# Three edits in a one-core attention and two-MLP kernel: left tiles 32 bytes lower, score matmuls of two heads by turns, seven conversion slots dropped

## The chip, the cores and the metric

The kernel runs on one core of a Trainium2 chip. The metric is the time of one execution on the device in microseconds, as the median of several runs. A core has TensorE (PE in the profile; its weight loads are PEld), VectorE (DVE), ScalarE (ACT), GpSimd (POOL) and SyncE (SP, which here issues nearly all DMAs).

## The reference

Windowed attention (window 64, causal), then two MLPs, all in float32. It is cut here to what is computed:

```python
# q, k, v: (4, 8, 576, 64)
scores = np.matmul(q, k.transpose(0, 1, 3, 2)) / np.sqrt(64)
mask = (rel >= 0) & (rel < 64)          # rel = query position - key position
attn = softmax(np.where(mask, scores, -1e9))
x = matmul(attn, v)                      # -> (2304, 512)
x = np.maximum(x @ w_in, 0.0) ** 2 @ w_out          # (512, 2048), (2048, 512)
h = x @ w_in2
out = np.where(h > 0, h, np.exp(np.minimum(h, 0)) - 1) @ w_out2
```

## The kernel before

Work goes by five blocks of tokens (512, 256, 512, 512, 512). Every large product is made of three matmuls of `fp32r` halves (high by high, high by low, low by high), so operands are kept as a high and a low part, which ScalarE (`gs<-g`, `xo<-xq`, copy of the high part) and VectorE (the low part) make.

**First stage** (to about 307 us): attention of all blocks, and the first MLP of the first three blocks in the direct way: `h_chunk` (TensorE `ph<-xs,w`) and `o_chunk` (TensorE `o<-gs,w`). All of it follows `ORDER1`, an order written out by hand; while `pinned` is set, every instruction is queued on its engine behind the one before. Heads come in pairs, head 0 in partitions 0 to 63 and head 1 in 64 to 127. The action `S` (and from the second block on `G`) makes the scores: `s_half` (L551) has for each quarter `i` of 128 queries two matmuls of 64 rows by 64 columns, one for each half window, with 128 columns moving, in full fp32. In the trace these are `pa<-kr,qd`, two rows for each call. In the first block an `S` is for one head, with its own place in the order; elsewhere `act_S` (L1101) calls `s_half` for head 0 and then for head 1, into two PSUM banks. VectorE (`R`), ScalarE (`E`) and the rest of the softmax follow per quarter.

**Second stage** (307 to about 436 us): the first MLP of the last two blocks by a Strassen scheme. `stepw(p, i)` makes product `i` of step `p` (8 steps, products 1, 2, 6, 5, 7, 4, 3) from `xo` and weights that `w0_load` fetches; TensorE rows are `px<-xo,w` (products 1, 6, 7, 4) and `py<-xo,w` (2, 5, 3), 6 matmuls each. Products 5 and 3 of a step go into the same bank, y: after 5 and 7 are done, VectorE adds bank y and the kept `tl` into `gb`, and only then may product 3 write the bank. `outw` (rows `o<-gs,w`, 12 matmuls) comes between, and from 436 to 476 us 14 of them without a break. The products' order on TensorE is fixed by `in_turn`; the other engines' order is made by a planner, except where `tc.issue_after` sets it.

**Third stage** (from 476 us): the second MLP by the same scheme on 384 columns, with rows `px`, `py`, `po`.

**Portions.** Meanwhile the weights of the second MLP have to be decoded from 8-byte words, summed and split. That is the generator `portions()` (L437): a chain of small steps on ScalarE (`top<-tl`, `wo<-y`, `tl<-y`) and VectorE (`y<-tl,top`, `y<-y`, `wo<-y,wo`, `tl<-y,tl`) through one buffer `y`, with fetches (`tl<-in_moe`) and stores (`wd<-wo`, `wd<-tl`) on SP's queue. It has 433 steps: 73 in its first loop, then 19 for each of eight tasks of the first weight matrix and 26 for each of eight of the second. `ORDER1` takes 215 of them one by one (`P.0` to `P.214`; the last 19 stand at its end, behind all of its matmuls). The other 218 are taken by `slot()` (L516), which runs steps to the next place where the generator gives a non-zero value, and queues them behind the last VectorE and ScalarE instruction of the step before. 43 slots use them up; 66 slots are called.

**Places.** Pools are laid from both ends of SBUF. From the left: `cst` (with the pad `pad2`), `wts`, then `at` and later `lw` and `la`. From the right: `pad`, then `sc`, `xp` and later `gb`. In bytes of a partition, the first tile behind `cst` (`top`) begins at 2848. Every operand of a large product on the left (`w`, `wr`, `xo`, and `g` of the third stage) begins a whole multiple of 512 bytes above that; on the right `xs` begins at 179968 and `gs` at 212736, and all operands there lie multiples of 512 bytes apart. 179968 - 2848 is 345 x 512 + 480.

Of the kernel before, what the change touches and what calls it, by code (L numbers as in the profile page):

```python
# [10 lines left out]
F32 = mybir.dt.float32  # L11
# [8 lines left out]
P = 128  # L20
WIN = 64
# [114 lines left out]
def window_attention_then_two_mlps(  # L136
# [37 lines left out]
    vec, act, pe = Noted(nc.vector, "cd"), Noted(nc.scalar, "ca"), Noted(nc.tensor, "pe")  # L174
# [13 lines left out]
    D = P // 2  # L188
# [12 lines left out]
    cst = ctx.enter_context(tc.tile_pool(name="cst", bufs=1))  # L201
# [6 lines left out]

    pad = pool(ctx, "pad", 1, side="right")
    pad.tile([P, 56], F32, name="pad")  # L210
    cst.tile([P, 32], F32, name="pad2")

    wts = pool(ctx, "wts", 1)
    ps_o = pool(ctx, "ps_o", 1, space=PSUM)
# [286 lines left out]
    def slot(n=1):  # L501
        with tc.issue_after(last["cd"].ins), tc.issue_after(last["ca"].ins):
            quiet.append(1)
            while True:
                x = next(todo, None)
                if x is None:
                    count[0] += 1
                if x != 0:
                    break
            quiet.pop()  # L510
# [38 lines left out]

    st = {}  # L550

    def s_half(u, a, ps):
        t, p = u
        qr, kr = raw[u]["q"], raw[u]["k"]
        d = slice(a * D, (a + 1) * D)
        for i in range(BLOCKS[t] // P):
            for c in range(2):
                o = (2 * i + c) * WIN
                pe.matmul(
                    out=ps[c * WIN:(c + 1) * WIN, i * P:(i + 1) * P],  # L560
                    lhsT=qr[d, o:o + WIN], rhs=kr[d, o:o + P], start=True, stop=True,
                )
        st.setdefault(u, {})["s", a] = ps

    def s_max(u, a, g):
        t, p = u
# [140 lines left out]
    order = [(t, p) for t in range(NB) for p in range(HP)]  # L707
# [143 lines left out]
    def bank(k):  # L851
        if k == "x":
            return among((0, 1), "px")
        if k == "a":
            return among((2, 3), "py")
        return ps_o.tile([P, 512], F32, tag=f"o{k}", name="po")
# [4 lines left out]
    def in_turn(fn, *a):  # L861
        with ExitStack() as line:
            for ins in behind2:
                line.enter_context(tc.issue_after(ins.ins))
            fn(*a)
        behind2[:] = [last["pe"]]
# [22 lines left out]
    def w0_load(m=1):  # L889
        for p, n in SEQW[wl0[0]:wl0[0] + m]:  # L890
            k = PROD[n][0]
            w = W[-1, p, k] = lw[0].tile([P, 2, HW], F32R, tag="ring", name="w0", bufs=10)
            sp.dma_start(out=w.bitcast(F32), in_=wd0[p][:, ORD1.index(k)])
        wl0[0] += m

    def square(g):
        act.activation(out=g, in_=g, func=AF.Relu)
        act.activation(out=g, in_=g, func=AF.Square)

    def ready(j, f):  # L900
        s = gw[j] = sc.tile([P, 2, NMAX], F32R, tag="gs", name="gs", bufs=GB)
        split(s[:, 0], s[:, 1], f, vec)

    def stepw(p, i):

        if i == 1:
            QW[p] = {"x": bank("x"), "done": set()}
        q = QW[p]
        k = "x" if i in (1, 6, 7, 4) else "z" if i == 2 else "y"
        if i in (2, 5):  # L910
            q[k] = bank("a")
        in_turn(prod, -1, p, i, q[k], i in (1, 2, 5), i in (4, 2, 3), NMAX)
        w0_load()
        q["done"].add(i)
        if i in (1, 6, 7):
            act.activation(out=tl[i], in_=q["x"], func=AF.Copy)
        if i == 2:
            f = sc.tile([P, NMAX], F32, tag="g", name="g")
            add(f, tl[1], q["z"])
            square(f)  # L920
            ready(p, f)
        if i == 4:
            f = sc.tile([P, NMAX], F32, tag="g", name="g")
            act.activation(out=f, in_=q["x"], func=AF.Relu)
            act.activation(out=f, in_=f, func=AF.Square)
            ready(p + NP, f)
        if i in (5, 7) and {5, 7} <= q["done"]:
            g = rest[p] = xp.tile([P, 2, NMAX], F32, tag=f"xs{p % KD}", name="gb")
            add(g[:, 1], tl[7], q["y"])
            square(g[:, 1])  # L930
        if i == 3:
            g = rest[p]
            add(g[:, 0], tl[6], q["y"])
            square(g[:, 0])
# [30 lines left out]
    def add(out, a, b):  # L965
        vec.tensor_tensor(out=out, in0=a, in1=b, op=ALU.add)
# [131 lines left out]
    def s_bank(g, n):  # L1098
        return ps_o.tile([P, 512], F32, tag=f"o{2 * (g % 2) + n}" if g < HP else f"b{2 + n}", name="pa")

    def act_S(g, *ns):  # L1101
        for a in ns or (0, 1):
            s_half(order[g], a, s_bank(g, a))

    def act_G(n):
        if HP + n < len(order):
            act_S(HP + n)
        if n > 1:
            s_V(order[HP + n - 2], spot(1, "pa"))
# [34 lines left out]
    def act_close():  # L1144
# [8 lines left out]
        "Lv": lambda g: u_load(order[g], "v"),  # L1153
        "Lw": w_load,
        "S": act_S,
        "R": lambda g, *a: s_max(order[g], *a),
        "E": lambda g, *a: s_exp(order[g], *a),
# [33 lines left out]
    pinned.clear()  # L1191
    behind2[:] = [last["pe"]]
    tl.update({k: lw[0].tile([P, NMAX], F32, tag=f"tl{k}", name="tl") for k in (1, 6, 7)})
    for i in (1, 2):
        stepw(0, i)
        slot()

    for i in (6, 5, 7):
        stepw(0, i)
        slot()  # L1200
    for p in range(1, NP):
        stepw(p, 1)
        slot()
        stepw(p, 2)
        slot()
        if p > 1:
            in_turn(outw, p - 2 + NP)
            slot()
        stepw(p - 1, 3)
        slot()  # L1210
        stepw(p, 6)
        slot()
        stepw(p - 1, 4)
        in_turn(outw, p - 1)
        slot()
        if p < NP - 1:
            stepw(p, 5)
            slot()
            stepw(p, 7)
        else:  # L1220
            stepw(p, 7)
            in_turn(outw, p - 1 + NP)
            slot()
            stepw(p, 4)
            stepw(p, 5)
            in_turn(outw, p)
            slot()
            stepw(p, 3)
            in_turn(outw, p + NP)
# [32 lines left out]
    for p in range(1, NP):  # L1262
        g = gb.tile([P, 4, NH], F32, name=f"gr{p}")
# [108 lines left out]
```

## Time and profile before

| | |
|---|---|
| median of 3 runs | 841.26 us (841.2 to 844.03) |
| profiled execution | 840.23 us |
| its span, first to last instruction | 838.4 us |
| TensorE busy | 819.9 us (98%) |
| VectorE busy | 603.7 us (72%) |
| ScalarE busy | 553.6 us (66%) |
| mean granted TensorE clock | 0.995 |

Busy time is a share of the span. Matmuls are pipelined: a row's length runs from the first start to the last (modelled) end, so the distance of starts tells how fast a stream goes, and the length of a group is that of its stream and one matmul's way through the array. A busy TensorE can still be slower than it might be.

### The profile page before, as it was taken

Reading aid. Unit: us, or ns where it says so; the run is one execution under the profiler, and the core shown is the slowest. Engines: PE = TensorE matmul, PEld = TensorE weight load, DVE = VectorE, ACT = ScalarE, POOL = GpSimd, SP = SyncE. Lnnn points to the kernel's source line nnn. Section 1 sums busy time; section 2 is a strip of 40 time slices with the busy share of each in tenths; the row PEclk is TensorE's granted clock in tenths of the full one; section 3 lists DMA queues with packets and bytes.
Section 4 is the critical chain, followed back from the end, with each engine's and each line's share of the span. In section 5 each row is a group of like instructions: output and inputs, shape, how many; then the busy total and the mean of one; then the engine's idle time right before and its main releaser. Section 6 shows DMA issues by size and latency. Waiting matters only on the chain.

```text
span 838.4 us, 14725 instructions
## 1 busy us (share of the span) xinstructions
PE 819.9 (98%) x5196; PEld 739.5 (88%) x5196; DVE 603.7 (72%) x1415; ACT 553.6 (66%) x1267; POOL 2.1 (0%) x11
## 2 busy tenths in 40 slices
PE   7999999999999996999999999999999999999997
PEld 6777789998888885788888899999999999999997
DVE  6998988774787666676676356699676798566874
ACT  6867666675777576787874357666477766477652
POOL 1000000000000000000000000000000000000000
PEclk9999999999999998999999999999999999999999
DMA  9980387674776668999957497878987886887832
GB/s 336 406 329 15 108 279 270 238 263 158 252 266 214 219 234 291 382 366 335 343 192 247 133 322 286 294 265 278 296 282 259 325 261 211 275 274 277 297 116 58
DMA packets 98682, 214.86 MB, mean 256 GB/s; under 512 B 26544, under 2 KB 53680, under 8 KB 90160
## 3 DMA queue, kind: packets, MB, share of 16 engines
q1 hardware_dynamic: 97776, 213.72, 73.4%
q8 instruction: 41, 0.67, 0.3%
q10 hardware_dynamic: 832, 0.20, 0.1%
q14 instruction: 33, 0.27, 0.1%
HBM read 160.41 MB, written 53.48 MB: 255 GB/s over the span
## 4 chain that ended last, share of the span: by engine, by line
PE 94%; DMA 2%; DVE 1%; ACT 1%; issue 1%; POOL 0%; SPq 0%; POOLq 0%; ACTq 0%
PE po L167 26%; PE o L167 24%; PE px L167 14%; PE ph L167 13%; PE py L167 9%; PE pa L167 8%; DMA tl<-in_moe_w_out_dram 1%; DVE pb L167 1%; DMA tl<-in_moe_w_in_dram 1%; DMA wd<-wo 1%; DMA w<-wd 0%; ACT top L167 0%; ACT gb L167 0%; ACT pb L167 0%; ACT wo L167 0%
## 5 line engine op out<-in xcount | busy, mean ns | idle before, releaser
L167 PE MATMUL o<-gs,w 128*128 128x512 f32 (+1 forms) x960 | 218.1, 375 | 0.0
L167 PEld LDWEIGHTS o<-gs,w 128*128 128x128 f32 x960 | 166.3, 188 | 33.1 <-issue 0.2
L167 PE MATMUL po<-g,wr 128*128 128x384 f32 (+1 forms) x972 | 168.6, 333 | 0.0
L167 PEld LDWEIGHTS po<-g,wr 128*128 128x128 f32 x972 | 167.4, 188 | 0.0
L167 ACT ACTIVATE g<-gr 128x384 fp32r<-128x384 f32 x168 | 87.2, 526 | 55.3 <-PE po L167 48.9
L167 PE MATMUL ph<-xs,w 128*128 128x512 f32 (+1 forms) x576 | 121.9, 359 | 1.3 <-ACT g L167 0.7
L167 PEld LDWEIGHTS ph<-xs,w 128*128 128x128 f32 x576 | 95.5, 188 | 19.4 <-ACT g L167 1.1
L167 DVE TENSOR_TENSOR g<-gr,g 128x384 fp32r<-128x384 f32 x168 | 90.0, 552 | 16.0 <-ACT g L167 14.9
L167 PE MATMUL px<-xo,wr 128*128 128x384 f32 x432 | 83.8, 334 | 0.0
L167 PEld LDWEIGHTS px<-xo,wr 128*128 128x128 f32 x432 | 75.8, 188 | 0.4
L167 DVE TENSOR_TENSOR gs<-g,gs 128x512 fp32r<-128x512 f32 (+1 forms) x64 | 39.8, 623 | 36.0 <-ACT gs L167 35.1
L167 ACT ACTIVATE sy<-px 128x384 f32<-128x384 f32 x69 | 33.8, 490 | 43.5 <-PE px L167 43.1
L167 ACT ACTIVATE g<-ph 128x512 f32<-128x512 f32 (+1 forms) x48 | 25.2, 525 | 52.9 <-PE ph L167 49.5
L167 ACT ACTIVATE pb<-pb,nm 128x128 f32<-128x128 f32 x144 | 55.8, 390 | 2.5 <-DVE nm L167 2.5
L167 PE MATMUL po<-xo,wr 128*128 128x384 f32 x288 | 56.2, 334 | 0.0
L167 PE MATMUL py<-xo,wr 128*128 128x384 f32 x288 | 55.7, 334 | 0.0
L167 DVE TENSOR_TENSOR gr<-sy,py 128x384 f32<-128x384 f32 x48 | 26.6, 554 | 37.4 <-PE py L167 24.1
L167 DVE TENSOR_TENSOR gr<-gr 128x384 f32<-128x384 f32 x96 | 52.1, 553 | 0.5
L167 PEld LDWEIGHTS po<-xo,wr 128*128 128x128 f32 x288 | 50.5, 188 | 0.0
L167 PEld LDWEIGHTS py<-xo,wr 128*128 128x128 f32 x288 | 50.4, 188 | 0.0
L167 PE MATMUL px<-xo,w 128*128 128x512 f32 x192 | 47.5, 395 | 0.0
L167 PE MATMUL py<-xo,w 128*128 128x512 f32 x144 | 38.4, 403 | 7.6 <-DVE gb L167 7.6
(89 smaller groups left out, 1099.3 us busy)
## 6 DMA issues: line engine op xcount, KB each, us to landing
wr<-wd SPq DMA_DIRECT2D x66, 1024.0 KB, 5.9
wr<-wd SPq DMA_DIRECT2D x24, 768.0 KB, 4.7
wd<-wo SPq DMA_DIRECT2D x28, 512.0 KB, 4.3
w<-wd SPq DMA_DIRECT2D x56, 256.0 KB, 5.1
wd<-tl SPq DMA_DIRECT2D x25, 512.0 KB, 4.7
vr<-in_v_dram SPq DMA_DIRECT2D x16, 512.0 KB, 5.2
wraw<-in_moe_w_in_dram SPq DMA_DIRECT2D x16, 511.8 KB, 9.8
wraw<-in_moe_w_out_dram SPq DMA_DIRECT2D x16, 511.8 KB, 9.3
```

What stands on the lines that cost most here:

```text
L167: r = fn(*a, **kw)
```

## The change

Three edits. The pad `pad2` shrinks by 32 bytes, and with it everything on the left behind it begins 32 bytes lower (`top` at 2816); the right side stays. `scores` takes the place of `s_half`: it goes through the quarters, and in each makes the matmuls of all the heads that it is given, so that both heads' matmuls come by turns; with one head (first block) the order is as before. In the second stage the slots behind the first seven products, (0, 1), (0, 2), (0, 6), (0, 5), (0, 7), (1, 1) and (1, 2), are gone. Their portions are taken by the slots that follow; 59 are left.

```diff
-    cst.tile([P, 32], F32, name="pad2")
+    cst.tile([P, 24], F32, name="pad2")
...
-    def s_half(u, a, ps):
+    def scores(u, banks):
         t, p = u
         qr, kr = raw[u]["q"], raw[u]["k"]
-        d = slice(a * D, (a + 1) * D)
         for i in range(BLOCKS[t] // P):
-            for c in range(2):
-                o = (2 * i + c) * WIN
-                pe.matmul(
-                    out=ps[c * WIN:(c + 1) * WIN, i * P:(i + 1) * P],
-                    lhsT=qr[d, o:o + WIN], rhs=kr[d, o:o + P], start=True, stop=True,
-                )
-        st.setdefault(u, {})["s", a] = ps
+            for a, ps in banks.items():
+                d = slice(a * D, (a + 1) * D)
+                for c in range(2):
+                    o = (2 * i + c) * WIN
+                    pe.matmul(
+                        out=ps[c * WIN:(c + 1) * WIN, i * P:(i + 1) * P],
+                        lhsT=qr[d, o:o + WIN], rhs=kr[d, o:o + P], start=True, stop=True,
+                    )
+        for a, ps in banks.items():
+            st.setdefault(u, {})["s", a] = ps
...
     def act_S(g, *ns):
-        for a in ns or (0, 1):
-            s_half(order[g], a, s_bank(g, a))
+        scores(order[g], {a: s_bank(g, a) for a in ns or (0, 1)})
...
-    for i in (1, 2):
+    for i in (1, 2, 6, 5, 7):
         stepw(0, i)
-        slot()
-
-    for i in (6, 5, 7):
-        stepw(0, i)
-        slot()
     for p in range(1, NP):
         stepw(p, 1)
-        slot()
+        if p > 1:
+            slot()
         stepw(p, 2)
-        slot()
+        if p > 1:
+            slot()
```

## Rows read from the trace of the kernel before

**Rows 1.** The page, part 1: busy us, share of the span, instructions of each engine.

```profile
PE 819.9 (98%) x5196; PEld 739.5 (88%) x5196; DVE 603.7 (72%) x1415; ACT 553.6 (66%) x1267; POOL 2.1 (0%) x11
```

**Rows 2.** By stretch: its length, each engine's busy us, TensorE's clock, DMA share, GB/s.

```profile
20.00:60.00 40.00, 38.34 (x290) 30.07 (x287) 37.37 (x83) 29.18 (x57) 0.00 (x0) 1.00 1.01 395
...
189.00:307.00 118.00, 118.00 (x916) 96.58 (x916) 80.91 (x239) 80.38 (x214) 0.00 (x0) 1.00 0.64 219
...
343.00:409.00 66.00, 66.00 (x289) 53.89 (x288) 43.35 (x102) 54.58 (x121) 0.00 (x0) 1.00 1.00 360
...
436.00:476.00 40.00, 40.00 (x174) 32.32 (x173) 20.64 (x28) 15.90 (x25) 0.00 (x0) 1.00 0.60 202
```

**Rows 3.** Timeline of TensorE, score groups: start, length in us, instruction, count.

```profile
22.80 1.09 PE L167 MATMUL pa<-kr,qd 64*64 64x128 f32 x16
...
74.41 0.68 PE L167 MATMUL pa<-kr,qd 64*64 64x128 f32 x16
...
178.01 1.59 PE L167 MATMUL pa<-kr,qd 64*64 64x128 f32 x32
```

**Rows 4.** Timeline of TensorE in the second and third stage, undisturbed groups of products.

```profile
334.81 2.88 PE L167 MATMUL px<-xo,w 128*128 128x512 f32 x12
337.53 1.52 PE L167 MATMUL py<-xo,w 128*128 128x512 f32 x6
...
436.20 39.36 PE L167 MATMUL o<-gs,w 128*128 128x512 f32 x168
475.40 0.51 PE L167 MATMUL px<-xo,wr 128*128 128x384 f32 x2
...
544.18 39.68 PE L167 MATMUL po<-g,wr 128*128 128x384 f32 x228
```

**Rows 5.** TensorE by shape, 60 to 476 us, then from 476 us: count | busy us, mean ns.

```profile
L167 PE MATMUL o<-gs,w 128*128 128x512 f32 x684 | 171.7, 399 | 0.0
L167 PE MATMUL ph<-xs,w 128*128 128x512 f32 x312 | 77.3, 396 | 0.7 <-ACT g L167 0.7
...
L167 PE MATMUL po<-g,wr 128*128 128x384 f32 x948 | 165.8, 334 | 0.0
L167 PE MATMUL px<-xo,wr 128*128 128x384 f32 x430 | 83.5, 334 | 0.0
L167 PE MATMUL po<-xo,wr 128*128 128x384 f32 x288 | 56.2, 334 | 0.0
L167 PE MATMUL py<-xo,wr 128*128 128x384 f32 x288 | 55.7, 334 | 0.0
```

**Rows 6.** Timeline of TensorE around product (0, 3), the first row; idle us and releaser bracketed.

```profile
324.18 2.93 PE L167 MATMUL py<-xo,w 128*128 128x512 f32 x6 [7.25 <-DVE gb L167]
326.90 3.88 PE L167 MATMUL px<-xo,w 128*128 128x512 f32 x12
...
333.43 1.55 PE L167 MATMUL py<-xo,w 128*128 128x512 f32 x6
```

**Rows 7.** Timeline of VectorE in the same stretch.

```profile
321.23 0.69 DVE L167 TENSOR_TENSOR wo<-y,wo 128x512 fp32r<-128x512 f32 x1 [1.59 <-ACT wo L167]
...
323.44 0.68 DVE L167 TENSOR_TENSOR gb<-tl,py 128x512 f32<-128x512 f32 x1
...
329.14 0.68 DVE L167 TENSOR_TENSOR tl<-y,tl 128x512 fp32r<-128x512 f32 x1
```

**Rows 8.** Timeline of ScalarE in the same stretch.

```profile
320.56 0.63 ACT L167 ACTIVATE wo<-y 128x512 fp32r<-128x512 f32 x1 [1.14 <-DMA wd<-wo]
```

**Rows 9.** By stretch, as rows 2, behind the start of product (0, 3).

```profile
326.00:328.00 2.00, 2.00 (x6) 1.58 (x5) 0.40 (x2) 0.93 (x3) 0.00 (x0) 0.50 0.49 178
```

**Rows 10.** Timeline of TensorE, product (1, 3).

```profile
342.17 1.67 PE L167 MATMUL py<-xo,w 128*128 128x512 f32 x6 [0.31 <-DVE gb L167]
```

**Rows 11.** Timeline of VectorE ahead of it.

```profile
340.98 0.43 DVE L167 SCALAR_TENSOR_TENSOR y<-tl,top 128x256 uint32<-128x256 uint32 x1 [2.57 <-ACT top L167]
341.43 0.69 DVE L167 TENSOR_TENSOR gb<-tl,py 128x512 f32<-128x512 f32 x1
```

## The prediction

> **What bounds the kernel now.** Read the engine totals first: TensorE is busy nearly all of the span [rows 1]. A second look, by stretches, shows where that holds: between 189 and 307 us, 343 and 409, and 436 and 476, TensorE has no idle time at all, while VectorE and ScalarE have a sixth to 60% of the time to spare [rows 2]. In such stretches only what shortens TensorE's own stream shortens the kernel. So the third look is at TensorE's rows in order of time, for two things: how far apart matmuls of the same shape start, and where the row says that the engine sat idle.
>
> **Part 1, score quarters by turns.** A score matmul uses 64 rows and 64 columns of the array, so four fit side by side: two heads (row halves) by two halves of a window (column halves). Each matmul of full fp32 shows as two in the trace. In the first block, where one head is scored by itself, 16 of them take 1.09 us: two abreast in 8 rounds [rows 3]. In the second block (256 tokens) the two heads' 16 take 0.68 us: four abreast in 4 rounds, although the program gives head 0 first [rows 3]. In the 512-token blocks the 32 of both heads take 1.59 us [rows 3], which is neither 8 rounds (about 1.1) nor 16 (about 2.2): the second head joins in only after several rounds of the first. By turns every round can hold four from the start, so 32 make 8 rounds; the nearest row for 8 rounds is the 1.09, and with 0.03 us for the second head's later start (an estimate; 0.1 us in its place would cost 0.8 us of the sum) it makes 1.12. That saves 1.59 - 1.12 = 0.47 us each. There are 12 such groups of 32 (three blocks by four pairs of heads), all in stretches without idle time: **-5.7 us**. Bounds: 0 (the queue gives no more overlap) and -9.5 (half of 1.59, twelve times). The four 256-token groups are four abreast already: 0. VectorE reads head 0's last quarter about when it did, since head 0's rounds were stretched by the overlap before; nothing waits for it soon.
>
> **Part 2, the left side 32 bytes lower.** It moves no work, so its price must be in TensorE's pitch. Two classes of 512-column matmuls stand in the trace. Products whose two operands both lie on the left start 226.7 ns apart (12 from 334.81 to 337.53 us); products with weights on the left and the moving operand on the right (gs, xs) start 233.3 ns apart (168 from 436.20 to 475.40 us) [rows 4]. By the addresses above, operands that are both on the left are a whole multiple of 512 bytes apart, operands on different sides are 32 bytes off one. After the move every pair is a multiple apart, 177152 = 346 x 512 bytes between the sides. If the distance of the two operands is what counts, the second class falls to 226.7. From 60 us on it has 684 + 312 = 996 matmuls [rows 5]: 996 x 6.67 ns = 6.6 us. Between 20 and 60 us TensorE still waits for others [rows 2], and I count nothing there. In the 436 to 476 us stretch each new gs comes from VectorE, which also makes the next stage's operands there; the 168 matmuls of that stretch are worth 1.1 us, of which I let 0.5 be lost. So **-6.1 us**, with bounds -6.6 below and, above, what the rivals say. The 256-column ones show no such two classes that I could price: 0.
>
> The Trainium skill speaks against this part (page "SBUF — State Buffer", sections "SBUF: two separate sides" and "Who interferes with whom"): lines are 16 bytes long, the moving operand and the weights have read ports of their own, and TensorE never waits on anyone there. 2848 and 2816 are both multiples of 16, so by that page the move is worth nothing. The trace's 233.3 against 226.7 ns at one shape is a difference for which the page has no place.
>
> **Part 3, seven portions later.** The most visible loss is TensorE's idle time of 7.25 us ahead of product (0, 3), at 324.18 us [rows 6]. It waits for the VectorE add that reads bank y (gb, 323.44). On VectorE that add is queued behind work on conversion steps, one of which (321.23) waited 1.59 us for ScalarE [rows 7], which itself had waited for a store to release its buffer [rows 8]. Are those steps the ones that the change moves? No. Counting the generator's steps (73 for the first loop, then 19 for each of the first eight tasks), everything that VectorE does there except the two steps of the products themselves is P.197 to P.211 of ORDER1, which the change leaves. The first instruction of a slot portion runs at 329.14 us [rows 7], after the stall. So I leave those 7.25 us in place, and with them the halved clock that follows: the granted clock is 0.50 at 326 to 328 us [rows 9].
>
> What the seven portions do hold up is the next round: the add at 341.43 us stands on VectorE behind a decode step (340.98) that sat 2.57 us for ScalarE [rows 11], and TensorE lost 0.31 us for it at 342.17 plus a slow restart (6 matmuls in 1.67 us, where the undisturbed 6 took 1.52) [rows 4, 10]. Gone: **-0.4 us** (bounds 0 and -0.5; -9.7 if the large stall goes, below). The moved portions issue ten DMAs on SP's queue (six stores, four fetches), now behind the loads of seven more products; those loads only come earlier. The cost of running later: 66 slots become 59, and 43 are needed, so the last portion falls from behind product (5, 3) to behind (6, 3), still inside the stage; ScalarE keeps 17% of its time there [rows 2]. If that cover is gone the portions run into the evictions at the stage's end, and the bank waits there cost what I would bound by the seven portions' VectorE time, some 15 operations of 0.43 to 0.69 us [rows 7, 11]: up to 8 us, in full only if nothing hides them. I take 0.
>
> **The sum.** -5.7 - 6.1 - 0.4 = -12.2 us. The profiled execution took 840.23 us (838.4 of span and 1.8 around it), which gives 828.0. The median of the runs is 841.26, 1.0 above the profiled one, and what is asked is a median: 841.26 - 12.2 = **829.0 us**.
>
> **Rivals.**
> The large stall goes too. The planner that orders the unpinned instructions puts the gb add behind P.211 although its inputs (tl and bank y) are there by 316 us; a small shift may let it in earlier. Then 7.25 us of waiting and the low clock go: 6 matmuls in 2.93 instead of 1.52 us, 12 in 3.88 instead of 2.88 [rows 4, 6], 2.4 us. 829.0 - 9.6 = 819.4 us. For it: the add waits for nothing on the chip but its place. Against it: nothing that the change removes stands ahead of it.
> The move gives nothing, because the right side itself or something else makes the 6.67 ns. Then 841.26 - 6.1 = 835.2 us. For it: weights are never on the right, so the trace never shows a right-hand product at the other distance. Against it: the slower pitch lingers for some matmuls into left-hand products that follow gs ones (the 6 at 333.43 take 1.55 against 1.52 us [rows 4, 6]), as an interplay of the two streams would. This is the result that the page cited above gives.
> Slower: the moving operand's own start counts, and starts at an odd multiple of 32 bytes are the fast ones. Left operands would then lose it. The last stage alone has 948 + 430 + 288 + 288 = 1954 left-left matmuls, now 173.3 ns apart at 384 columns (228 in 39.68 us) [rows 4, 5]; at 6.67 ns more that is 13.0 us against the 6.1 gained: 848.2 us. It decides for slower from 6.1 us / 1954 = 3.1 ns a matmul on. Against it: it would make the well-aligned start the bad one.
>
> **How the numbers follow.** The forecast (829.0) 0.50; the stall goes as well (819.4) 0.20; the move gives nothing (835.2) 0.17; the reverse (848.2) 0.08; portions colliding at the end of the stage, with all else as forecast (some 833 to 837) 0.05. The forecast, the move that gives nothing and most of the case without the stall lie between 818 and 836: about 0.8. A measurement here can tell some 0.5% from no change, 4.2 us. Below 837.05: 0.86; within 4.2 us of 841.26: 0.05; above 845.5: 0.09.
>
> **What would show it.** After: groups of 32 score matmuls near 1.12 us; o rows of 168 in some 38.2 us instead of 39.36 and of 12 in 2.88; the last stage's pitch still 173.3; the wait ahead of (0, 3) still about 7 us, the one ahead of (1, 3) gone; wait rows on TensorE between 60 and 300 us still next to nothing. It is wrong if gs rows keep 233.3, if left-left rows leave 226.7 and 173.3, if TensorE sits idle around 432 to 440 us, or if the stall changes by more than 2 us.

## The result, and the profile after

The changed kernel takes 833.77 us (median of 4 runs, 829.09 to 834.96) where the kernel before, run beside it, takes 841.41 us: a ratio of 0.9892, with a 95% interval of 0.9848 to 0.9936. It is faster, by 7.6 us between the medians, where 12.2 were forecast; 829.0 us was said, with a range of 818 to 836. The four runs spread over 5.9 us, and the profiled execution is the longest of them, 834.96 us, with a span of 833.2, so it shows more waiting than the median.

TensorE's busy time on the page, which answers [rows 1]:

```profile
PE 809.5 (97%) x5196; PEld 732.7 (88%) x5196; DVE 602.8 (72%) x1415; ACT 551.9 (66%) x1267; POOL 2.1 (0%) x11
```

TensorE's stream is 10.4 us shorter than 819.9, but it is now busy 97% instead of 98%: something that was not there before makes it wait. The stretches say where; the columns are those of [rows 2]. First the one stretch of before that [rows 2] leaves out, then three after.

```profile
409.00:436.00 27.00, 27.00 (x119) 21.97 (x118) 18.37 (x43) 20.31 (x45) 0.00 (x0) 1.00 0.72 262
```

```profile
343.00:409.00 66.00, 63.92 (x281) 52.22 (x280) 41.62 (x99) 49.42 (x111) 0.00 (x0) 1.00 0.96 335
409.00:436.00 27.00, 25.70 (x111) 20.34 (x110) 18.73 (x42) 20.55 (x45) 0.00 (x0) 1.00 0.69 252
436.00:476.00 40.00, 38.87 (x174) 32.00 (x173) 19.85 (x27) 15.44 (x24) 0.00 (x0) 1.00 0.54 185
```

In before TensorE had no idle time between 343 and 476 us; now it loses 2.1, 1.3 and 1.1 us in these three stretches. The work in them is 5 to 11 us further on than in before, which changes nothing in that reading. The timeline of TensorE after, columns as in [rows 3, 6]:

```profile
110.85 1.10 PE L167 MATMUL pa<-kr,qd 64*64 64x128 f32 x32
...
173.95 1.10 PE L167 MATMUL pa<-kr,qd 64*64 64x128 f32 x32
...
314.79 2.93 PE L167 MATMUL py<-xo,w 128*128 128x512 f32 x6 [7.18 <-DVE gb L167]
317.52 3.20 PE L167 MATMUL px<-xo,w 128*128 128x512 f32 x12
...
331.44 1.52 PE L167 MATMUL py<-xo,w 128*128 128x512 f32 x6
...
339.33 1.66 PE L167 MATMUL py<-xo,w 128*128 128x512 f32 x6 [0.94 <-DVE gb L167]
...
380.50 1.66 PE L167 MATMUL py<-xo,w 128*128 128x512 f32 x6 [2.00 <-DVE gb L167]
...
420.46 3.02 PE L167 MATMUL o<-gs,w 128*128 128x512 f32 x12 [1.29 <-ACT gs L167]
...
451.49 3.01 PE L167 MATMUL o<-gs,w 128*128 128x512 f32 x12 [0.93 <-DVE gs L167]
```

The groups of 32 score matmuls take 1.10 us, all twelve of them, where [rows 3] had 1.59. The stall ahead of product (0, 3), now at 314.79, is what it was in [rows 6]. The wait ahead of (1, 3) of [rows 10] is gone (331.44 starts without one). New are the waits at 339.33 (product (2, 5)), 380.50 (product (4, 3)), 420.46 (the `outw` behind product (7, 7)) and 451.49 (among the last 14 `outw`).

The one at 380.50 can be followed back. VectorE, then ScalarE in the same stretch:

```profile
376.50 0.43 DVE L167 TENSOR_TENSOR y<-y 128x256 f32<-128x256 f32 x1
379.76 0.69 DVE L167 TENSOR_TENSOR gb<-tl,py 128x512 f32<-128x512 f32 x1 [2.84 <-ACT tl L167]
```

```profile
378.80 0.49 ACT L167 ACTIVATE top<-tl 128x256 f16<-128x256 bf16 x1 [2.79 <-DMA tl<-in_moe_w_out_dram]
379.16 0.57 ACT L167 ACTIVATE tl<-px 128x512 f32<-128x512 f32 x1
```

Read it from the back: TensorE waits for the gb add (379.76); that waits for ScalarE's copy of bank x (379.16); and the copy waits for nothing of its own, it stands in ScalarE's queue behind a decode step (378.80) that sat 2.79 us until its fetch had landed. A conversion step stands in front of an eviction (the copy that frees a PSUM bank), and holds up TensorE. That fetch was issued at 371.55 and took 7.17 us to land; the other 26 fetches of this weight matrix that were issued between 330 and 440 us took 2.6 to 6.8.

The wait at 339.33 begins in the same way, over five us ahead of it. ScalarE, then VectorE:

```profile
333.80 0.50 ACT L167 ACTIVATE top<-tl 128x256 f16<-128x256 bf16 x1 [4.34 <-DMA tl<-in_moe_w_out_dram]
...
335.99 0.63 ACT L167 ACTIVATE gs<-g 128x512 fp32r<-128x512 f32 x1
```

```profile
336.65 0.69 DVE L167 TENSOR_TENSOR gs<-g,gs 128x512 fp32r<-128x512 f32 x1 [1.90 <-ACT gs L167]
...
338.60 0.68 DVE L167 TENSOR_TENSOR gb<-tl,py 128x512 f32<-128x512 f32 x1
```

The decode step sat 4.34 us for its fetch, the split of gs stands behind it on ScalarE, VectorE waits for that, and the gb add that TensorE needs stands behind it on VectorE.

The one at 420.46 is of another kind. It waits for a gs that is made from product (6, 4), whose bank was complete at 414.82. ScalarE:

```profile
415.69 0.63 ACT L167 ACTIVATE gb<-gb 128x512 f32<-128x512 f32 x1 [0.83 <-DVE gb L167]
416.23 0.40 ACT L167 ACTIVATE wo<-y 128x256 fp32r<-128x256 f32 x1
416.54 0.48 ACT L167 ACTIVATE top<-tl 128x256 f16<-128x256 bf16 x1
...
417.88 0.58 ACT L167 ACTIVATE g<-px 128x512 f32<-128x512 f32 x1
...
419.79 0.62 ACT L167 ACTIVATE gs<-g 128x512 fp32r<-128x512 f32 x1
```

The bank is read at 417.88 only, 3.1 us late, behind conversion steps and the square of a sum that VectorE had made late. ScalarE waits for no fetch between 409 and 420 us.

### The profile page after: what moved, and what is told of

Same layout as the page of the kernel before. It is cut to its first block, busy times and chain, and to the rows that moved or that the text cites. A ratio compares the mean times of both kernels' runs of the same rounds, so it can differ in the third digit from the quotient of the medians.

```text
span 833.2 us, 14722 instructions
## 1 busy us (share of the span) xinstructions
PE 809.5 (97%) x5196; PEld 732.7 (88%) x5196; DVE 602.8 (72%) x1415; ACT 551.9 (66%) x1267; POOL 2.1 (0%) x11
## 4 chain that ended last, share of the span: by engine, by line
PE 79%; DMA 9%; DVE 5%; ACT 5%; issue 2%; SPq 0%; POOL 0%; ACTq 0%; POOLq 0%; DVEq 0%
PE po L167 26%; PE o L167 16%; PE ph L167 13%; PE px L167 10%; PE pa L167 7%; PE py L167 6%; DMA tl<-in_moe_w_out_dram 4%; DMA x2d<-ev 1%; DVE y L167 1%; DMA top<-in_moe_w_out_dram 1%; ACT g L167 1%; ACT gb L167 1%; DVE wo L167 1%; ACT top L167 1%; DMA xq<-x2d 1%
## 5 line engine op out<-in xcount | busy, mean ns | idle before, releaser
L167 PE MATMUL o<-gs,w 128*128 128x512 f32 (+1 forms) x960 | 215.3, 373 | 2.4 <-ACT gs L167 1.3
L167 PE MATMUL ph<-xs,w 128*128 128x512 f32 (+1 forms) x576 | 120.1, 357 | 1.4 <-ACT g L167 0.7
```

Of the source, the lines that this page charges most:

```text
L167: r = fn(*a, **kw)
```

## The experiments

Two theories stood at the start. **A**: the move and the turns pay as forecast, and the dropped slots cost what is missing. **B**: the slots are innocent; a faster TensorE runs ahead of the weight conversion and waits for it, whatever made it faster. Four kernels tell them apart, each part alone and the first two together.

### The move alone

```diff
-    cst.tile([P, 32], F32, name="pad2")
+    cst.tile([P, 24], F32, name="pad2")
```

> The kernel before with the left side 32 bytes lower and nothing else; the order on every engine is that of before. Theory A (the move pays by itself, and what the changed kernel lost comes from the dropped slots): the 168 o matmuls from 436 us start 226.7 ns apart instead of 233.3, about 841.4 - 6.6 = 834.8 us, and TensorE's waits on gb stay at 7.6 us in 2. Theory B (what it lost comes from TensorE running ahead of the weight conversion, with whatever slots): part of the 6.6 is given back as new waits on gb or gs between 340 and 476 us, 837 to 840 us.

836.25 us against 841.05 beside it (0.9942, interval 0.9928 to 0.9955): -4.8 us. TensorE's timeline and then its waits, from 300 us on (us in total, times, longest):

```profile
431.86 20.11 PE L167 MATMUL o<-gs,w 128*128 128x512 f32 x88
```

```profile
PE py L167 <- DVE gb L167: 8.0, 2, 7.7
PE o L167 <- DVE gs L167: 0.9, 2, 0.7
```

88 matmuls in 20.11 us, of which the last one's way through the array is 0.39: 19.72 / 87 = 226.7 ns, against the 233.3 of [rows 4]. The pitch does what theory A says. Of the gain, 0.9 us goes into new waits on gs at the end of the stage, where gs became the later one, and 0.4 into gb. That is a little of B, and more than the 0.5 us that the prediction had set aside; the time is A's.

### The turns alone

```diff
-        for a in ns or (0, 1):
-            s_half(order[g], a, s_bank(g, a))
+        scores(order[g], {a: s_bank(g, a) for a in ns or (0, 1)})
```

> The kernel before with the score quarters by turns and nothing else. Theory A: twelve groups of 32 score matmuls take 1.10 us instead of 1.59, 841.4 - 12 x 0.49 = 835.5 us, waits on gb as before. Theory B: part is given back as new waits between 340 and 476 us, 837 to 840 us.

835.74 us (0.9933, 0.9919 to 0.9947): -5.3 us. The groups take 1.10 us:

```profile
175.31 1.10 PE L167 MATMUL pa<-kr,qd 64*64 64x128 f32 x32
```

12 x 0.49 = 5.9 us by the rows; in the profiled execution the gb wait ahead of (1, 3) is 1.30 us instead of 0.31, a little of B. The time is that of theory A.

### The dropped slots alone

```diff
-    for i in (1, 2):
-        stepw(0, i)
-        slot()
-
-    for i in (6, 5, 7):
+    for i in (1, 2, 6, 5, 7):
         stepw(0, i)
-        slot()
     for p in range(1, NP):
         stepw(p, 1)
-        slot()
+        if p > 1:
+            slot()
         stepw(p, 2)
-        slot()
+        if p > 1:
+            slot()
```

> The kernel before without the slots behind the first seven products and nothing else. Theory A (dropping them costs, because the planner lays the whole second stage anew and conversion steps now wait for their fetches in front of evictions): waits on gb and gs appear between 340 and 476 us and the time is 843 to 847 us. Theory B (the dropped slots are innocent): 841.0 us, the wait ahead of (1, 3) gone and none new.

844.9 us (1.0048, 1.0031 to 1.0065): +3.9 us, slower. TensorE's waits from 300 us on:

```profile
PE py L167 <- DVE gb L167: 7.0, 1, 7.0
PE o L167 <- ACT gs L167: 1.0, 1, 1.0
PE o L167 <- DVE gs L167: 0.9, 1, 0.9
```

Before has the gb waits alone, 7.6 us in 2. The wait ahead of (1, 3) goes here too, as forecast, and two waits on gs come in its place, both late in the stage; new waits on gb, which theory A had named too, do not come:

```profile
428.04 3.06 PE L167 MATMUL o<-gs,w 128*128 128x512 f32 x12 [0.97 <-ACT gs L167]
...
459.59 4.64 PE L167 MATMUL o<-gs,w 128*128 128x512 f32 x17 [0.86 <-DVE gs L167]
```

By the time it is theory A.

### Move and turns, with all slots

The changed kernel with the slots put back (the diff above the other way).

> The changed kernel with the slots behind the first seven products put back (move and turns alone). Theory A (the dropped slots cost): 841.4 - 6.6 - 5.9 = 828.9 us, faster than the changed kernel's 833.8. Theory B (TensorE ahead of the conversion): about 834 us, with new waits on gb and gs between 340 and 476 us like those of the changed kernel.

829.64 us, 829.47 to 829.77 in its runs (0.9865, 0.9851 to 0.9879): -11.4 us, and 4.1 us below the changed kernel's median. With 841.05 - 4.8 - 5.3 = 830.9 the two parts add up. **Theory A stands, B falls**: a TensorE that is as fast as the changed kernel's waits 9.1 us from 300 us on (before: 7.6, changed: 12.5), as long as the slots stay. The 4.1 by itself is not clear of noise: the interval of the changed kernel, 0.9848 to 0.9936, holds the 0.9865. One of its four runs, 829.09, loses nothing against this kernel, and the other three lose 3.3 to 5.3 us. That seven dropped slots cost is shown by the slots alone, whose interval lies above 1. As the program is the same in every run, the order that it fixes is not all that decides; a slow fetch, as the one above, could be such a thing, but no second run of it was profiled.

### How do the dropped slots cost?

The slots alone don't only move seven portions. In the kernels with the move or the turns the order of VectorE, ScalarE and SP behind the first stage is that of before; with the seven slots gone the planner lays all three anew to the stage's end. Starts of the same product in us, from the timelines:

| | before | slots alone | move and turns | five slots dropped | changed (seven) |
|---|---|---|---|---|---|
| (0, 3) | 324.18 | 324.40 | 315.56 | 314.78 | 314.79 |
| (1, 3) | 342.17 | 342.35 | 333.20 | 331.57 | 331.44 |
| (2, 3) | 357.48 | 357.52 | 348.50 | 346.64 | 348.05 |
| (4, 3) | 387.83 | 388.17 | 378.42 | 376.56 | 380.50 |
| (7, 3) | 434.81 | 436.49 | 424.66 | 422.83 | 428.76 |
| third stage | 475.40 | 478.77 | 465.25 | 463.85 | 470.25 |

Up to (1, 3) the changed kernel is 1.8 us ahead of the one with all slots; by the third stage it is 5.0 behind. Of these 6.8 us, 3.8 are lost up to (4, 3), in the waits at 339.33 and 380.50, and 2.9 behind it, in the waits on gs. The slots alone lose only in that last part: they are 0.3 us behind at (4, 3), 1.7 at (7, 3) and 3.4 at the third stage. Two theories for the loss: **G**, lateness of the conversion costs by itself, slot for slot; **H**, the new order costs, where it puts decode steps ahead of evictions before their fetch has landed. The column of five dropped slots is the next experiment, on move and turns with only the five slots of step 0 dropped:

```diff
+    for i in (1, 2, 6, 5, 7):
         stepw(0, i)
```

> Move and turns, with only the five slots of step 0 dropped (behind (0, 1), (0, 2), (0, 6), (0, 5), (0, 7)). Theory G (conversion steps that run later cost by themselves, in proportion to the slots dropped, 4.1 us for seven): 829.6 + 2.9 = 832.5 us. Theory H (what costs is the order that the planner then lays: decode steps placed ahead of evictions before their fetch has landed): not in proportion, anywhere between 829 and 834, and it goes with ScalarE's waits on fetches, 9 us or less of them where it costs nothing, 11 us or more where it costs.

829.14 us (0.9861, 0.9848 to 0.9875): five dropped slots cost nothing. Then only the two behind (1, 1) and (1, 2):

```diff
-        slot()
+        if p > 1:
+            slot()
```

> Move and turns, with only the two slots behind (1, 1) and (1, 2) dropped; VectorE's and ScalarE's order is nearly that with all slots (19 and 21 lines of difference). Theory G: 829.6 + 1.2 = 830.8 us. Theory H: the order hardly differs, so 829.6 us, with ScalarE's waits on fetches as with all slots.

829.59 us (0.9866, 0.9853 to 0.9880): nothing either, though here G's 830.8 lies inside the interval. With five dropped it lies outside (832.5 / 841.37 is 0.9895, above the interval's 0.9875): that is no price by the slot, and G falls. ScalarE's waits on these fetches between 300 and 436 us, for the changed kernel, all slots, and five dropped, in this order:

```profile
ACT top L167 <- DMA tl<-in_moe_w_out_dram: 11.1, 5, 4.3
```

```profile
ACT top L167 <- DMA tl<-in_moe_w_out_dram: 7.8, 6, 3.4
```

```profile
ACT top L167 <- DMA tl<-in_moe_w_out_dram: 4.8, 3, 2.2
```

Before has 5.3 us of them in 6, two dropped 6.8 in 5, the slots alone 9.1 in 4. The two kernels that lose time are the two with the most, though the 9.1 is below the 11 that was given as the mark. That, and the chains at 333.80 and 378.80, speak for H. But H is not the whole account. The slots alone have 9.1 us of these waits and lose nothing to them up to (4, 3); their loss, like the last 2.9 us of the changed kernel's, comes from waits on gs at the stage's end, and the one at 420.46 has no fetch in front of it (with the slots alone, one decode step that waited 1.09 us, at 422.80, does stand ahead of the same copy). With all slots the same copy of (6, 4) stands among as many conversion steps and starts 1.0 us behind its bank instead of 3.1:

```profile
413.61 0.58 ACT L167 ACTIVATE g<-px 128x512 f32<-128x512 f32 x1
```

The sum of (6, 3), which stands ahead of it, is made 0.6 us behind its product there and 2.9 in the changed kernel; why it is late was not followed further. Closer to the loss than ScalarE's waits on fetches are VectorE's waits for ScalarE's decode step `top`: 17.8 us in the changed kernel and 18.8 with the slots alone, 8.9 to 11.5 in the other four. So it is shown that the seven slots cost, and where TensorE waits; that a fetch in front of an eviction does it is shown for the waits at 339.33 and 380.50, which lie in the 3.8 us of the changed kernel. Why the waits on gs come is open. The rest is a correlation over six kernels: a kernel with the new order but with the fetches there in time was not made.

### The large stall

The prediction left the 7.25 us ahead of (0, 3) in place, because VectorE's add is queued behind P.197 to P.211. Here these and the three behind them leave the written order (on move and turns with all slots), and the slots take them:

```diff
-... X.17 P.196 P.197 P.198 P.199
-P.200 ... P.214
+... X.17 P.196
```

> Move and turns with all slots of before, and the last 18 conversion steps (P.197 to P.214) no longer at the end of the first stage's written order but taken by the slots. Theory E (the 7.7 us ahead of product (0, 3) come from the gb add's place behind these steps): that wait and the low clock behind it go, 829.6 - 7.7 - 2.4 = 819.5 us, if nothing comes back. Theory F (the weight conversion is bound by its transfers from 320 to 430 us, and TensorE running 10 us earlier only meets it elsewhere): the waits on gb and gs between 330 and 470 us grow by most of it, 826 to 830 us.

820.95 us (0.9759, 0.9743 to 0.9774): -8.7 us against the 829.64. TensorE, then VectorE:

```profile
305.91 1.52 PE L165 MATMUL py<-xo,w 128*128 128x512 f32 x6
308.99 1.67 PE L165 MATMUL py<-xo,w 128*128 128x512 f32 x6 [1.56 <-DVE gb L165]
310.50 2.91 PE L165 MATMUL px<-xo,w 128*128 128x512 f32 x12
```

```profile
307.92 0.42 DVE L165 TENSOR_TENSOR tl<-y,tl 128x256 fp32r<-128x256 f32 x1
308.26 0.68 DVE L165 TENSOR_TENSOR gb<-tl,py 128x512 f32<-128x512 f32 x1
```

The add now runs at 308.26, right behind ScalarE's copy that it reads (its end, 308.06) and ahead of most of these steps. Of 7.7 us of stall 1.6 are left, and no low clock follows: the granted clock is 1.00 at 309 to 313 us, and the 12 px matmuls take 2.91 us, where [rows 6] had 3.88. Theory E. The conversion does not meet TensorE later, as F had it, though its last steps (from 424.87 on VectorE) come some 9 us behind the last product (from 415.76 on TensorE). With the five slots of step 0 dropped as well, it ends still later:

> Move and turns, the last 18 conversion steps left to the slots, and the five slots of step 0 dropped: the conversion is then the latest of all against TensorE. Theory G (lateness costs): 820.95 + 2.9 = 823.9 us or more, with waits at the end of the stage. Theory H (order, not lateness): costs only where ScalarE waits on a fetch with an eviction behind it; near 821 us if those waits stay small.

818.61 us (0.9738, 0.9723 to 0.9753), no slower than the 820.95 (the intervals overlap), with the conversion's end 13 us behind the last product's. Lateness at the end of the stage costs nothing here; G falls a second time.

### Distance or start?

Four kernels like before but for the pads. **C**: the distance between the two operands counts. **D**: the start of a side by itself counts. First the right side moved instead of the left:

```diff
-    pad.tile([P, 56], F32, name="pad")
+    pad.tile([P, 48], F32, name="pad")
```

> The kernel before with the right side 32 bytes higher (pad of 48 floats instead of 56; left at 2848, right at 180000), nothing else: the two sides are a multiple of 512 bytes apart, 346 x 512, as in the changed kernel, but each starts at an odd multiple of 32 bytes. Theory C (the distance of the two operands counts): o and ph matmuls of 512 columns go from 233.2 to 227.7 ns, 256-column ones from 118.4 to 119.9, time about 836.3 us as with the left side moved. Theory D (the start of the left side, or of either side by itself, at a multiple of 64 counts): nothing changes, 233.2 ns and 841 us, or slower.

```profile
432.21 20.11 PE L167 MATMUL o<-gs,w 128*128 128x512 f32 x88
```

835.88 us (0.9936, 0.9919 to 0.9954): the same 226.7 ns and the same gain, with both sides at odd multiples of 32 bytes. Then both sides moved (`pad` 48 and `pad2` 24), which leaves the left start at a multiple of 64 and takes the distance 32 bytes past 346 x 512:

> The kernel before with both moves (left at 2816, right at 180000): the left side starts at a multiple of 64, and the sides are 32 bytes off a multiple of 512. Theory C (distance): the gain is undone, o and ph matmuls of 512 columns at about 233 ns, time near 841 us. Theory D (the left side's own start): 227.7 ns and 836 us.

```profile
436.68 20.95 PE L167 MATMUL o<-gs,w 128*128 128x512 f32 x88
```

842.22 us, one run, where before takes 841.19. The row holds two breaks, of 0.16 and 0.11 us; the undisturbed starts of this stage (161 distances) are 233.3 ns apart on the mean. The gain is gone. C stands, D falls. Then `pad2` of 28, 16 bytes short of the multiple:

> The kernel before with the left side only 16 bytes lower (2832): 16 bytes off a multiple of 512. Theory C with a sharp bound (only the exact multiple is good): 233 ns. Theory C by degrees (half the way off, half the price): about 230 ns. Theory D (left start at a multiple of 64): 233 ns.

```profile
435.93 20.70 PE L167 MATMUL o<-gs,w 128*128 128x512 f32 x88
```

840.87 us, one run; 20.31 / 87 = 233.4 ns, the full price for half the way. And `pad2` of 8, 64 bytes past the multiple:

> The kernel before with the left side 96 bytes lower (2752): the two sides are then 346 x 512 + 64 bytes apart. If a multiple of 64 bytes between the operands is enough: 512-column o and ph matmuls at 227.7 ns and about 836 us, as with a multiple of 512. If it must be a larger power of two up to 512: 233 ns and about 841 us.

```profile
432.72 20.32 PE L167 MATMUL o<-gs,w 128*128 128x512 f32 x88
```

837.43 us (0.9957, 0.9943 to 0.9971): 19.93 / 87 = 229.1 ns, between the two. Neither of the two expectations: 64 bytes is better than 16 or 32, and not as good as the multiple of 512. The distances between 64 and 512 were not tried.

## Why the prediction was right, and where it was not

| term of the sum | forecast | measured |
|---|---|---|
| scores by turns | -5.7 | -5.3 alone (12 x 0.49 = 5.9 by rows) |
| left side lower | -6.1 | -4.8 alone (-5.3 with the right side moved instead) |
| both | -11.8 | -11.4 |
| seven slots | -0.4 | +3.9 alone; +4.1 on top of the others, not clear of noise |
| stall ahead of (0, 3) | stays, 7.25 us | stays, 7.18 us |
| sum | -12.2 | -7.6 |

**Scores.** Right in mechanism and size: 8 rounds, 1.10 us where 1.12 was taken from the first block's row. (12 x 0.47 is 5.6; the sum carries 5.7.)

**The move.** Right in mechanism, the distance of the two operands. The size was a little too large for two reasons that the rows of before could not show. The undisturbed stream runs at 226.7 ns as forecast, but matmuls next to other work keep 231 to 236, so that the mean of the undisturbed starts over the whole trace fell from 233.3 to 227.6 ns (o) and from 233.1 to 227.5 (ph): some 5.6 ns on 996 matmuls, not 6.67. And "the 256-column ones: 0" was wrong by a little the other way: they went from 118.4 to 119.9 ns, 384 matmuls, about +0.6 us. The 0.5 us set aside for gs was 0.9. The rival "the move gives nothing", which is what the Trainium skill gives (page "SBUF — State Buffer", sections "SBUF: two separate sides" and "Who interferes with whom": TensorE never waits on anyone there), falls with the trace: 226.7 against 233.3 ns at one shape, by 32 bytes. The reverse rival falls too; the last stage keeps 173.3 ns in every kernel here.

**The slots.** This is the step that failed, by 4.3 to 4.5 us, and it is nearly the whole difference between 829.0 and 833.8. That 833.8 still lies in the range of 818 to 836 is owed to the other two parts, not to this one, whose sign was wrong. What it said of the portions themselves held: they are not those of the large stall, the wait ahead of (1, 3) went, and running later is covered. What it did not say is that the order of the other instructions is not fixed: "those loads only come earlier" and "I take 0" hold for an order written by hand, while here a planner lays everything behind the first stage, and dropping seven slots gave it another plan. The rival that named collisions at the end of the stage (833 to 837, chance 0.05) came out with the right time and with part of the place: 2.9 of the 6.8 us, and all that the slots alone lose, come behind (4, 3), in waits on gs. The other 3.8 come in the stage's middle, where fetches that land late stand in front of evictions, which the prediction did not have. And it is not lateness that collides: conversions that end 9 and 13 us behind the last product cost nothing.

**The large stall.** Its cause and its price were read rightly (9.6 us for the wait and the low clock; 8.7 were gained when the steps ahead of the add were taken away), and so was the conclusion that the change doesn't touch it.

## What to carry to other kernels

Where a planner orders the queues, the price of taking a step away is not only the step: compare the order of every engine before and after, and ask which wait now stands in front of an eviction. Here conversion steps that ran 9 and 13 us late cost nothing, while one that stood in front of an eviction before its fetch had landed cost TensorE 2.0 us. Look at the pitch of undisturbed rows by where their operands lie: two classes at one shape are a gain that no busy share shows.

## What the runs showed of the hardware

The pitch of a 512-column fp32r matmul depends on the distance between its two operands: a mean of 226.8 to 227.3 ns at 346 x 512 bytes (eight kernels), 229.1 at 64 bytes more, and 233.3 at 16 less, 32 less and 32 more (undisturbed starts among the 168 o matmuls that end the second stage). At 256 columns it goes the other way: a mean (o matmuls) of 119.9 ns at the multiple, 118.4 at 16 and 32 bytes less, 117.2 at 32 more and 117.8 at 64 more. How many matmuls of 64 x 64 run abreast depends on their order in the program: the same 32 took 1.10 us by turns, four abreast, and 1.59 head by head, while groups of 16 were four abreast in either order (0.67 and 0.68 us).
